# Load pieces of 256 KB and a reordered schedule in a fused attention and feed-forward kernel

## The chip, the cores and the metric

The kernel runs on one core of a Trainium2 chip. The metric is the device time of one execution in microseconds (us). A ratio between two kernels is the mean time of one kernel's fast runs over the mean time of the other's fast runs of the same rounds, so it is not quite the ratio of the medians quoted beside it. Each run is slow when it took over 1.5% more than the fastest run of the same kernel, else fast. The medians and ranges quoted are of all runs; three slow ones of the experiments are in them (a_128k 273.18, a_perm 249.43, a_tok_warm 245.64). Stretches and waits are read from one profiled execution of each kernel, which was fast except for a_128k; the span is its length.

Engines in the profile: PE is the matrix engine's matmuls, PEld its weight loads, DVE the vector engine, ACT the scalar engine, POOL the third elementwise engine, SP the engine that issues loads. A name with a q, such as ACTq, is that engine's sequencer as it issues DMAs. PEclk is the clock that the throttle granted to PE, 1.00 being full speed.

## The reference, cut to what matters

```python
# q, k, v: [4 batches, 8 heads, 768 tokens, 64], lam: [8]
for each block of 64 tokens:                       # linear attention with decay lam
    intra = (q k^T * decay mask) v
    inter = (q * lam^(pos+1)) kv_state
    out   = intra + inter
    kv_state = lam^64 * kv_state + (k * decay)^T v
x = out as [3072 tokens, 512]                      # heads side by side
h = x @ w_in                                       # [3072, 2048]   "GEMM1"
g = h + sin(alpha * h)^2 / (alpha + 1e-9)
y = g @ w_out                                      # [3072, 512]    "GEMM2"
```

## The kernel before

The kernel takes the 3072 tokens in six chunks of 512. A chunk needs four attention steps (a step is 128 tokens of two batches, four heads), 16 groups of GEMM1 and 16 groups of GEMM2. A group is four matmuls of 128x128 by 512 columns, 0.865 us at full clock. Step s reads q, k and v that SP loads as fp32; DVE and POOL scale q and k by powers of lam and round to bf16 (`prep_x`), ACT or POOL rounds v (`prep_v`); PE transposes q and k, forms the scores, and forms the output together with the running state; POOL rounds the state to bf16 (`Zs`); ACT stores the step's output as `xT`, the input of GEMM1.

The host program does not fix the order of instructions by hand. It records every operation with its reads, its writes and an assumed duration, plays them through a model of the five engines, and emits each engine's instructions in the order of the model. The program of each engine is this fixed list.

A load in the kernel before brings half of the heads of one tensor for one batch, 128 KB in packets of 512 bytes:

```python
def load(s, what="kqv", after=()):
    pair, n, hh = where(s)
    ...
    for nme in what:
        for u in range(2):                                   # two batches
            off = (((2 * pair + u) * H + HS * hh) * S + n * BL) * D
            a = bass.AP(src.tensor, off, [[2 * D, 64], [S * D, HS], [1, 2 * D]])
            op = rec_load(lambda e, ...: e.dma_start(d[half(u), :, :], a), ..., 117500, after)
```

The model of the kernel before assumes 0.25 us for an issue of SP and a rate of 270 GB/s for the loads (`issue = {"SP": 0.25, ...}`, `rate=270e3`).

The attention step works on tiles of 64 rows. The Trainium skill ("TensorEngine Tiling (Array Packing)", section "Restrictions and Gotchas", Gotcha 1) says that different row tiles cannot access the same PSUM bank at once and that software must synchronise. The kernel orders the parts of a step with fences (a fence makes a part wait until an earlier part has finished); a step has three parts in the kernel before:

```python
seqs = [block(first), block(mid), block(second)]    # cut: which matmuls go where
...
    if i == 2 and fence is not None:
        op.fence = fence                             # the third part waits for the first
```

A finished output tile of GEMM2 (128 tokens, 512 columns, 256 KB) is copied by ACT and stored with one DMA. Partition 64t+i of the tile holds token 2i+t, so the outermost dimension of the store has size 2:

```python
dst = bass.AP(out.tensor, row0 * DM, [[DM, 2], [2 * DM, 64], [1, DM]])
rec("ACT", lambda e: e.dma_start(dst, osb[o][:, :]), ...)
```

The main part, cut:

```python
for m in range(NM):
    grp_A(0, m, "ACT" if m % 5 == 4 else "POOL")              # GEMM1 of chunk 0
prep_step(4)
for i in range(16):                                           # GEMM2 of chunk 0, steps 4 to 7
    if i in B0_SEC: sec(...)
    grp_B(0, ...)
for m in range(NM):                                           # GEMM1 of chunk 1
    if m == 10: steady(6, "ACT")                              # attention inside a GEMM1 phase
    ...
for bi, (c, s4, m4) in enumerate(b_seq):                      # the rest: GEMM2, GEMM1 and attention in turns
    grp_B(c, s4, 4 * m4, 4, bank)
    for _ in range(...):
        grp_A(ca, m, ...)
        if ai % 4 == 1: steady(...)
```

Of the kernel before, what the change touches and what calls it, by code (L numbers as in the profile page):

```python
# [14 lines left out]
class Op:  # L15
    __slots__ = ("eng", "fn", "deps", "dur", "idx", "sem_after", "slot", "kslot",
                 "pos", "users", "start", "end", "nbytes", "clock", "prio", "signal", "soft", "soft_users", "fence")

    def __init__(self, eng, fn, dur, idx):
        self.eng, self.fn, self.dur, self.idx = eng, fn, dur, idx  # L20
        self.deps = set()
        self.soft = ()
        self.fence = None
        self.slot = None
        self.kslot = 0
        self.signal = False
        self.prio = idx


class Program:  # L30



    ENGINES = ("PE", "DVE", "ACT", "POOL", "SP")

    def __init__(self):
        self.ops = []
        self.writer = {}
        self.readers = {}
        self.slots = {}  # L40

    def add(self, eng, fn, dur, reads=(), writes=(), slot=None, nbytes=0, after=(), prio=None, soft=()):
        op = Op(eng, fn, dur, len(self.ops))
        if prio is not None:
            op.prio = prio
        self.ops.append(op)
        op.nbytes = nbytes
        for b in reads:
            w = self.writer.get(b)
            if w is not None:  # L50
                op.deps.add(w)
            self.readers.setdefault(b, []).append(op)
        for b in writes:
            w = self.writer.get(b)
            if w is not None and w is not op:
                op.deps.add(w)
            for r in self.readers.get(b, ()):
                if r is not op:
                    op.deps.add(r)
            self.writer[b] = op  # L60
            self.readers[b] = []
        for a in after:
            op.deps.add(a)
        op.deps.discard(op)
        op.soft = tuple(soft)
        if slot is not None:
            op.slot = slot
            self.slots[slot] = self.slots.get(slot, 0) + 1
            op.kslot = self.slots[slot]
        return op  # L70

    def schedule(self, hop=0.1, rate=270e3, begin=1.2, done=1.2):
        issue = {"SP": 0.25, "POOL": 0.8, "ACT": 0.5}
        for op in self.ops:
            op.users = []
            op.soft_users = []
        for op in self.ops:
            for d in op.deps:
                d.users.append(op)
            for d in op.soft:  # L80
                d.soft_users.append(op)
        left = {op: len(op.deps) + len(op.soft) for op in self.ops}
        ready_at = {op: 0.0 for op in self.ops}
        free = {e: 0.7 for e in self.ENGINES}
        pend = {e: [] for e in self.ENGINES}
        dma_free = 0.0
        pe_seq = [op for op in self.ops if op.eng == "PE"]
        pe_at = 0
        for op in self.ops:
            if not left[op]:  # L90
                pend[op.eng].append(op)
        order = []
        n = len(self.ops)
        while len(order) < n:
            best = None
            for e in self.ENGINES:
                if e == "PE":
                    if pe_at >= len(pe_seq):
                        continue
                    op = pe_seq[pe_at]  # L100
                    if left[op]:
                        continue
                    cand = (max(free[e], ready_at[op]), op)
                else:
                    if not pend[e]:
                        continue
                    t0 = min(max(free[e], ready_at[o]) for o in pend[e])
                    op = min((o for o in pend[e] if max(free[e], ready_at[o]) <= t0 + 1e-9),
                             key=lambda o: (o.prio, o.idx))
                    cand = (t0, op)  # L110
                if best is None or (cand[0], cand[1].idx) < (best[0], best[1].idx):
                    best = cand
            assert best is not None, "order and dependencies disagree"
            t, op = best
            e = op.eng
            if e == "PE":
                pe_at += 1
            else:
                pend[e].remove(op)
            op.start = t  # L120
            if op.slot is not None:
                free[e] = t + issue[e]
                if op.nbytes < 10000:
                    op.end = t + 2.9
                else:
                    dma_free = max(dma_free, t + begin) + op.nbytes / rate
                    op.end = dma_free + done
            else:
                op.end = t + op.dur
                free[e] = op.end  # L130
            order.append(op)
            for u in op.soft_users:
                left[u] -= 1
                ready_at[u] = max(ready_at[u], op.start)
                if not left[u] and u.eng != "PE":
                    pend[u.eng].append(u)
            for u in op.users:
                left[u] -= 1
# [74 lines left out]
def bass_lightning_attn__then__act_snake_kernel(  # L213
# [14 lines left out]
    BL = 128  # L228
# [16 lines left out]
    with es:  # L245
# [66 lines left out]
        def hold_bank():  # L312
            return idle.pop(0)
# [508 lines left out]
```

## Time and profile before

The kernel before took 280.06 us (median of three runs, 279.18 to 281.51). The span of its profiled execution is 277.9 us.

The table splits the span by what PE works on. All starts and ends are those of weight loads on PE in the trace. "Middle" is everything between GEMM1 of chunk 0 and GEMM1 of chunk 1: GEMM2 of chunk 0 and attention steps 4 to 7. "Steady" goes from the end of GEMM1 of chunk 1 to the last matmul, "tail" from there to the end of the span.

| stretch, us | before |
|---|---|
| until GEMM1 of chunk 0 | 25.6 |
| GEMM1 of chunk 0 | 16.2 |
| middle | 36.2 |
| GEMM1 of chunk 1 | 26.4 |
| steady | 156.8 |
| tail | 16.6 |

The page of the kernel before, the part with the span in 40 equal slices (one slice is 6.9 us, counted from 0 here); digits are tenths:

```profile
PE   0446999494592686978979999999999999999600
PEclk9999999959589599899999999999999999999975
GB/s 134 190 166 167 206 196 188 182 186 193 178 172 147 168 199 200 172 192 163 181 43 5 35 21 30 32 39 32 27 31 33 35 38 40 38 38 44 51 51 45
```

PE is full from slice 21 on. Before that it has holes, and in three slices its clock is at half speed. All DMA together moves 147 to 206 GB/s in slices 1 to 19; at the end the output runs at 51 GB/s with PE idle.

The view by windows of the kernel before: window, length, busy time (count) of PE, PEld, DVE, ACT and POOL, granted clock, share of the DMA engines' time, GB/s.

```profile
5.00:26.00 21.00, 8.96 (x336) 7.29 (x338) 9.52 (x14) 8.21 (x15) 13.23 (x17) 1.00 0.83 174
78.00:105.00 27.00, 18.61 (x144) 8.15 (x146) 11.22 (x17) 13.68 (x22) 14.05 (x14) 0.85 0.60 176
158.00:167.00 9.00, 8.56 (x122) 4.21 (x122) 6.95 (x10) 5.07 (x9) 5.97 (x6) 1.00 0.07 20
262.00:277.00 15.00, 0.00 (x0) 0.00 (x0) 0.00 (x0) 0.50 (x1) 0.00 (x0) 0.66 0.13 51
```

In the second line PE works 18.6 of 27 us. In the last line the DMA share of 0.13 is about two engines of sixteen.

The view of waits of the kernel before: who waits for whom, total us, times, longest us.

```profile
DVE q L409 <- DMA q<-in_q_dram: 30.7, 9, 6.3
ACT v L418 <- DMA v<-in_v_dram: 26.5, 12, 6.7
PEld PS L629 <- DVE gT L642: 15.7, 11, 7.1
```

DVE and ACT wait for loads, and PE then waits for DVE's GEMM1 results (gT) that stand behind those waits. The source line of the loads, first 24 us of the kernel before (duration of an issue in ns: least, median, most):

```profile
L333 SPq DMA_DIRECT2D k<-in_k_dram x8: 601/617/714, 0.7 to 9.4; - x8
```

One issue of 128 KB takes 0.617 us on SP, which is 0.66 us from issue to issue, so SP can ask for no more than 199 GB/s.

### The profile page before, as it was taken

The page shows a single profiled execution, that of the slowest core. Times are in us where ns is not written, and L with a number is a line of the kernel's source. Part 1 is how long each engine was busy: PE and PEld are TensorE (multiplying, and loading weights), DVE is VectorE, ACT ScalarE, POOL GpSimd, SP SyncE. Part 2 cuts the span into 40 slices and gives each one's busy share as a digit, 9 for nine tenths or more (in the row PEclk, how much of TensorE's full clock was granted, in tenths as well). Part 3 has the DMA queues.
Part 4 walks back from the last instruction along what each step waited for, and adds up shares of the span by engine and source line. Part 5 has one row for each costly group of instructions (what it writes and reads, how often), then busy time and mean ns, then how long its engine had stood idle before and what let it go on. Part 6 is the DMA issues. An engine that isn't in the chain of part 4 may idle for free.

```text
span 277.9 us, 6346 instructions
## 1 busy us (share of the span) xinstructions
PE 215.0 (77%) x2755; PEld 107.1 (39%) x2785; DVE 131.2 (47%) x181; ACT 132.0 (48%) x212; POOL 121.8 (44%) x137
## 2 busy tenths in 40 slices
PE   0446999494592686978979999999999999999600
PEld 0334444252340243543535445444444444444200
DVE  3552385332301578756778775466653444440000
ACT  5224684322433564576656566544556555541100
POOL 4656595212644463524665664344434344430000
PEclk9999999959589599899999999999999999999975
DMA  4679996666654667665610100011000111111111
GB/s 134 190 166 167 206 196 188 182 186 193 178 172 147 168 199 200 172 192 163 181 43 5 35 21 30 32 39 32 27 31 33 35 38 40 38 38 44 51 51 45
DMA packets 47243, 29.78 MB, mean 107 GB/s; under 512 B 2656, under 2 KB 44144, under 8 KB 47216
## 3 DMA queue, kind: packets, MB, share of 16 engines
q1 hardware_dynamic: 39168, 18.88, 24.1%
q0 software_dynamic: 4752, 4.19, 9.7%
q10 hardware_dynamic: 3296, 6.30, 6.7%
q8 instruction: 22, 0.36, 0.5%
q14 instruction: 5, 0.04, 0.0%
HBM read 27.28 MB, written 6.29 MB: 121 GB/s over the span
## 4 chain that ended last, share of the span: by engine, by line
PE 48%; DMA 14%; SPq 14%; DVE 11%; POOL 3%; issue 2%; ACT 2%; ACTq 0%; DVEq 0%
PE PS L652 20%; PE PS L629 19%; SPq L333 14%; DMA w<-in_moe_w_out_dram 7%; DMA q<-in_q_dram 5%; DVE gT L642 4%; PE PS L437 3%; DVE S_m L614 3%; PE PS L459 2%; DMA v<-in_v_dram 2%; DVE qkT L609 2%; PE PS L446 2%; POOL w L395 1%; POOL u L640 1%; DVE Zacc L587 1%
## 5 line engine op out<-in xcount | busy, mean ns | idle before, releaser
L640 POOL TENSOR_TENSOR u<-t 128x512 bf16<-128x512 bf16 x74 | 78.1, 1063 | 87.7 <-ACT t L633 87.5
L629 PE MATMUL PS<-xT,w 128*128 128x512 bf16 x375 | 97.0, 394 | 13.7 <-DVE gT L642 10.5
L652 PE MATMUL PS<-w,gT 128*128 128x512 bf16 x363 | 94.7, 395 | 4.3 <-issue 3.4
L642 DVE SCALAR_TENSOR_TENSOR gT<-u,r_sb,PS 128x512 bf16<-128x512 bf16 x96 | 69.9, 745 | 52.5 <-POOL u L640 45.9
L633 ACT ACTIVATE t<-PS,alpha_sb 128x512 bf16<-128x512 f32 x96 | 65.1, 686 | 55.0 <-PE PS L629 54.1
L629 PEld LDWEIGHTS PS<-xT,w 128*128 128x128 bf16 x384 | 37.7, 101 | 63.4 <-DVE gT L642 15.7
L652 PEld LDWEIGHTS PS<-w,gT 128*128 128x128 bf16 x384 | 37.0, 101 | 45.8 <-issue 5.7
L409 POOL TENSOR_TENSOR k<-k,Lk 128x512 bf16<-128x512 f32 x23 | 24.0, 1043 | 24.0 <-DMA k<-in_k_dram 18.6
L409 DVE TENSOR_TENSOR q<-q,Lq 128x512 bf16<-128x512 f32 x20 | 17.0, 850 | 33.1 <-DMA q<-in_q_dram 30.7
L614 DVE TENSOR_TENSOR S_m<-PS,mask 128x1024 bf16<-128x1024 f32 x24 | 29.1, 1218 | 4.8 <-PE PS L446 1.8
L418 ACT CAST v<-v 128x512 bf16<-128x512 f32 x24 | 14.9, 620 | 29.8 <-DMA v<-in_v_dram 26.5
L459 PE MATMUL PS<-S_m,v 64*64 64x128 bf16 x384 | 18.6, 248 | 10.0 <-ACT xT L596 5.9
L437 PE MATMUL PS<-ident,q 64*64 64x64 bf16 x384 | 14.3, 205 | 13.6 <-DVE q L409 6.8
L659 ACT COPY osb<-PS 128x512 f32<-128x512 f32 x24 | 13.9, 578 | 15.4 <-PE PS L652 15.3
L596 ACT CAST xT<-PS 128x512 bf16<-128x512 f32 x24 | 14.1, 587 | 11.4 <-DVE Zacc L587 9.5
L437 PEld LDWEIGHTS PS<-ident,q 64*64 64x64 bf16 x384 | 10.3, 116 | 23.7 <-issue 8.1
L446 PE MATMUL PS<-qkT 64*64 64x128 bf16 x384 | 18.0, 241 | 0.5 <-ACT qkT L611 0.4
L611 ACT COPY qkT<-PS 128x1024 bf16<-128x1024 bf16 x11 | 11.1, 1013 | 14.2 <-PE PS L437 13.4
L459 PEld LDWEIGHTS PS<-S_m,v 64*64 64x64 bf16 x384 | 11.5, 120 | 14.5 <-ACT xT L596 7.2
L587 DVE TENSOR_TENSOR Zacc<-PS,Zacc 128x256 f32<-128x256 f32 x16 | 6.8, 424 | 16.6 <-PE PS L437 12.3
L639 ACT ACTIVATE u<-t 128x512 bf16<-128x512 bf16 x22 | 13.8, 629 | 0.6
L437 PE MATMUL PS<-ident,k 64*64 64x64 bf16 x384 | 14.0, 203 | 0.0
(38 smaller groups left out, 103.6 us busy)
## 6 DMA issues: line engine op xcount, KB each, us to landing
k<-in_k_dram SPq DMA_DIRECT2D x48, 128.0 KB, 3.1
q<-in_q_dram SPq DMA_DIRECT2D x48, 128.0 KB, 3.4
v<-in_v_dram SPq DMA_DIRECT2D x48, 128.0 KB, 3.4
out_dram<-osb ACTq DMA_DIRECT2D x24, 256.0 KB
w<-in_moe_w_out_dram POOLq DMA_DIRECT2D x4, 512.0 KB, 17.2
w<-in_moe_w_in_dram POOLq DMA_DIRECT2D x3, 512.0 KB, 10.3
w<-in_moe_w_in_dram POOLq DMA_DIRECT2D x2, 256.0 KB, 6.4
lam_bc<-in_lam_dram ACTq DMA_DIRECT2D x1, 4.0 KB, 2.6
```

The source lines that it names most:

```text
L333: op = rec_load(lambda e, a=a, d=dst[r], u=u: e.dma_start(d[half(u), :, :], a), [f"{nme}32.{r}.{u}"], f"{nme}{r}", 117500, after)
L409: rec(eng, lambda e: e.tensor_tensor(dst[c][:, :, :], s_in, L_b, ALU.mult), 0.63 if eng == "DVE" else 1.05, reads=[f"{x}32.{r}.0", f"{x}32 ...
L418: rec("ACT", lambda e: e.copy(v2[c][:, :, :], v32[r][:, :, :].rearrange("p h (t d) -> p (h t) d", t=2)), 0.62, reads=[f"v32.{r}.0", f"v32. ...
L437: last = e.transpose(dst, src[half(u), hid(h, tt), :], ident[half(u), half(u)])
L446: return e.matmul(PS[half(u), sb_ + r, (h // 2 * 2 + tj) * 128:(h // 2 * 2 + tj + 1) * 128], qt[half(r), u, 1, h // 2, half(tj)], qt[half( ...
L459: return e.matmul(dst, v2[o % RC][half(u), hid(h, tj), :], S_m[o % RS][half(u), h % 2 ^ u, h // 2, tj, :], start=start, stop=True, skip_gr ...
L614: rec("DVE", lambda e: e.tensor_tensor(S_m[s % RS][:, :, :, :, :].rearrange("p r a t i -> p (r a) (t i)"), PS[:, sb_:sb_ + 2, :].rearrange ...
L629: last = e.matmul(PS[:, i, :], w1[:, kc, 128 * m:128 * (m + 1)], xT[x][:, kc, :], start=(kc == 0), stop=(kc == NKC - 1))
L633: rec("ACT", lambda e: e.activation(t16[tt][:, :], PS[:, i, :], ACTF.Sin, scale=alpha_sb[:, m:m + 1]), 0.7, reads=bk(i) + ["alpha"], write ...
L640: return e.tensor_tensor(u16[tt][:, :], t16[tt][:, :], t16[tt][:, :], ALU.mult)
L642: rec("DVE", lambda e: e.scalar_tensor_tensor(out=gT[g][:, m, :], in0=u16[tt][:, :], scalar=r_sb[:, m:m + 1], in1=PS[:, i, :], op0=ALU.mul ...
L652: last = e.matmul(PS[:, bank, :], gT[g][:, m, 128 * s4:128 * (s4 + 1)], w2[:, m, :], start=(m == 0), stop=(m == NM - 1))
```

## The change

Its intent is to feed PE better in the first 100 us and to waste less of the steady part.

1. A load brings all eight heads: 256 KB per DMA, half as many DMAs; SP's issue is assumed to take 0.66 us.
2. The attention step is cut into five parts around its fences instead of three.
3. Each chunk's GEMM1 is one phase on up to eight PSUM banks (PSUM is the memory that matmuls write); attention stands only in GEMM2 phases. Three of the 16 GEMM2 groups of a chunk move into the next chunk's GEMM1 phase.
4. The model that orders the instructions may now place an operation in an earlier gap of DVE, ACT or POOL (`probe`), and picks the engine that would finish first (`fastest`).

The output is left as it is. No arithmetic is taken out. The core of the diff, with cuts:

```diff
-    RL = 8
+    RL = 4
-        q32 = ring("q32", RL, [128, HS, 2 * D], F32)
+        q32 = ring("q32", RL, [128, H, 2 * D], F32)          # the same for k32, v32
 ...
-                a = bass.AP(src.tensor, off, [[2 * D, 64], [S * D, HS], [1, 2 * D]])
+                a = bass.AP(src.tensor, off, [[2 * D, 64], [S * D, nh], [1, 2 * D]])   # nh = 8
 ...
-            seqs = [block(first), block(mid), block(second)]
+                blocks = [(Ts[0] + Is[1], keys_t + keys_o, None), (Is[0] + Zz[1] + Es[1], keys_o, None),
+                          (Ts[1] + Zz[0] + Es[0] + Ss[0], keys_t + keys_o + keys_s, 0), (Ss[1], keys_s, None),
+                          (Ds[0] + Ds[1], keys_o, 2)]
 ...
+    ISSUE = {"SP": 0.66, "POOL": 0.8, "ACT": 0.66}
+    HOP, RATE, BEGIN, DONE = 0.1, 270e3, 1.2, 1.2
+    def place(self, eng, t, dur):
+        ...
+        t = self.probe(eng, t, dur)                          # first gap that is long enough
 ...
-        for bi, (c, s4, m4) in enumerate(b_seq):
-            grp_B(c, s4, 4 * m4, 4, bank)
-            for _ in range(0 if bi < START else 2 if bi in EXTRA else 1):
-                    grp_A(ca, m, "ACT" if m % 4 == 3 else "POOL")
+        for c in range(NCH):
+            for m in range(NM):
+                grp_A(c, m, every if m < 12 else ..., (SQ.get(m, "POOL"),))
+                if c > 0 and m in (3, 7, 11):
+                    grp_B(c - 1, 3, m // 4 + 1, low)
+            for i, (s4, m4) in enumerate(b_seq):
+                grp_B(c, s4, m4, ...)
+                if c > 1 and i in SEC: steady(4 * (c + 1) + SEC[i])
```

## The prediction

> **What bounds it now.** The measured 280.06 us splits, by the timeline of PE, into five stretches: 26.0 us to the first GEMM1 matmul; 78.8 us for GEMM1 of chunk 0, GEMM2 of chunk 0 with attention steps 4 to 7, and GEMM1 of chunk 1 (until 104.8); 157 us of interleaved GEMM1, GEMM2 and attention until the last matmul at 261.9; 16 us of output transfer after it; 2 us outside the span.
>
> - Stretch 2 holds 48 groups of four matmuls (0.865 us each, 41.5 us) and about 7 us of attention; about 26 us is waiting. Waits of DVE on q, ACT on v and POOL on k are 31, 27 and 19 us, longest 6 to 8 us, and the in-order engines hold up GEMM1 work queued behind them. The cause is the load queue: the SP timeline shows 0.66 us per 128 KB issue (199 GB/s) until 137 us, while a 512-byte packet takes 27 ns on one of 16 engines (303 GB/s). Loads are issue-bound.
> - Stretch 3 is PE-bound from 140 us (table by windows: PE 90 to 99% busy, clock 1.00). One period (4 GEMM1 and 4 GEMM2 groups, one attention step) is 8.76 us: 6.92 of groups, 1.64 of attention, 0.26 waiting for DVE.
> - The tail is output: 51 GB/s, DMA share 0.12, that is 2 of 16 engines; 5.1 us per 256 KB. The Trainium skill ("DMA: Bandwidth & Descriptors", section on why a DMA increments its semaphore by 16) says that the slowest dimension sets how many engines share a DMA; here it is 2. The change leaves this alone.
>
> **What changes.** No arithmetic is removed.
>
> 1. 256 KB loads: I expect the issue to stay near 0.66 us, so loads become transfer-bound at 0.87 us per piece, 303 GB/s. Weights start when v of the first block lands, about 12.5 us instead of 17.3. First GEMM1 matmul about 19.5 (saves 6.5).
> 2. Weights still need about 23.5 us, so the loads gated on them restart near 37; q for steps 4 and 5 lands about 7.5 us later. GEMM2 of chunk 0 waits some 4 us there, but the loads then stay ahead. GEMM1 of chunk 1 starts about 58.5 (78.5 before), GEMM2 of chunk 1 about 75 (104.8 before).
> 3. From there: 80 GEMM2 and 64 GEMM1 groups, 124.5 us; 18 attention steps, some partial, at 1.45 us (the five parts hide about 0.2 us of drain per step), 24 us; about 4.5 us of waits, where a phase begins or an ACT qkT copy (1.01 us after a 0.59 us xT copy) meets the next step 1.7 us later. GEMM1 phases take about 16.4 us; ACT is near 14 of it, so it should keep up. Last matmul about 228.
> 4. Tail unchanged, 16 us: four tiles of 5.1 us, the first finished 7.8 us before the end. Plus 2.
>
> Sum: 75 + 153 + 16 + 2 = **246 us**, range 236 to 257. Chances: faster by over 2% 0.97, within 2% 0.02, slower 0.01.
>
> **What would show it.** SP issue below 0.87 us, load bandwidth near 300 GB/s before 60 us; DVE waits on q below 10 us; first GEMM1 matmul near 19.5; GEMM1 of chunk 1 in about 16.5 us at clock 1.00; attention step 1.4 to 1.5 us; last matmul about 16 us before the end.
>
> **What would make it wrong.** If issue time grows with the piece (1.24 us for 256 KB), loads gain nothing: about 255. If waits of several us in GEMM2 of chunk 0 leave the clock low (matmuls at 0.43 instead of 0.216 us, as at 26 to 31 us before), add 3. If the fixed engine orders, set by assumed durations, meet late data, GEMM1 phases stretch and add 1 to 2 us per chunk. If the waits vanish, 238.

## The result and the profile after

The changed kernel took **261.02 us** (median of four runs, 260.82 to 261.4) against 279.62 of the kernel before; the ratio of the fast runs is 0.9325, 95% interval 0.9278 to 0.9372. That is faster, by 18.6 us, but 15 us slower than predicted and outside the range of 236 to 257. The result is correct; the span is 259.0 us.

| stretch, us | before | predicted | after | after less predicted |
|---|---|---|---|---|
| until GEMM1 of chunk 0 | 25.6 | 19.5 | 23.8 | +4.3 |
| GEMM1 of chunk 0 and middle | 52.4 | 39.0 | 49.6 | +10.6 |
| of this: GEMM1 of chunk 0 | 16.2 | | 14.4 | |
| of this: middle | 36.2 | | 35.3 | |
| GEMM1 of chunk 1 | 26.4 | 16.5 | 18.0 | +1.5 |
| steady | 156.8 | 153 | 150.3 | -2.7 |
| tail | 16.6 | 16 | 17.2 | +1.2 |

The prediction gave the points 19.5, 58.5, 75 and 228, from which the column follows. It named no length for the middle alone. With GEMM1 of chunk 0 as long as in the kernel before, 16.2, it leaves 39.0 - 16.2 = 22.8 us for the middle; the expectations below use that number. So the middle missed by 12.5 us. It is nearly as long as before although it holds less: 13 groups of GEMM2 instead of 16 (2.6 us). The other three stand in GEMM1 of chunk 1, where parts of two attention steps stood before.

The page after, the same three lines (one slice is 6.5 us):

```profile
PE   0448897299589999999999999999999999999400
PEclk9999999658959999999999999999999999999955
GB/s 138 226 166 172 206 206 188 227 228 220 99 154 194 224 193 186 229 134 143 97 157 150 53 51 21 34 12 49 51 17 42 3 43 51 31 40 18 51 51 44
```

PE is full from slice 12 on instead of 21. Slices 7 to 11 (45 to 78 us) hold a nearly empty one and a half-empty one, and the clock falls to half in two of them. Where loads run alone they reach 220 to 228 GB/s, not the predicted 303. The same windows after, moved with the stretches:

```profile
5.00:24.00 19.00, 9.41 (x338) 7.77 (x339) 10.84 (x16) 7.36 (x14) 11.72 (x15) 1.00 1.14 189
73.00:92.00 19.00, 18.56 (x77) 7.97 (x78) 12.14 (x19) 13.47 (x22) 11.41 (x12) 0.88 0.92 194
158.00:167.00 9.00, 9.00 (x124) 4.50 (x123) 6.80 (x10) 4.93 (x9) 5.15 (x6) 1.00 0.10 32
242.00:258.00 16.00, 0.32 (x2) 0.00 (x0) 0.00 (x0) 0.59 (x1) 0.00 (x0) 0.59 0.13 51
```

GEMM1 of chunk 1 is now PE-bound (18.56 of 19 us, with the clock at half until 77.5 us), the steady part has no waits left (9.00 of 9.00 against 8.56), and the tail is what it was. The DMA share in the first line rose from 0.83 to 1.14 while the rate rose only from 174 to 189 GB/s: more packets are under way at once, and each takes longer. From 5 to 24 us the median time of a 512-byte packet went from 27 to 42 ns in the traces.

The loads' source line after, first 24 us:

```profile
L298 SPq DMA_DIRECT2D k<-in_k_dram x4: 619/672/901, 0.7 to 4.2; - x4
L298 SPq DMA_DIRECT2D v<-in_v_dram x4: 1002/1082/1420, 7.4 to 11.0; - x4
```

The first issues of 256 KB take about as long as those of 128 KB did. The later ones take 1.08 us, which reads as the queue holding SP back: from 46 us on an issue comes every 1.12 us, and 256 KB in that time is 234 GB/s, close to the 228 that the window from 44 to 50 us shows below.

The waits after:

```profile
DVE q L381 <- DMA q<-in_q_dram: 10.0, 5, 4.8
PE PS L406 <- DVE q L381: 17.2, 3, 9.6
PE PS L428 <- POOL Zs L549: 3.2, 1, 3.2
PEld PS L577 <- DVE gT L591: 2.0, 8, 0.4
```

DVE waits 10 us for q instead of 30.7, and the weight loads of GEMM1 wait 2.0 us for gT instead of 15.7. What is left for PE is in the middle. Three views of the middle of the changed kernel follow. First the windows, then PE's two waits in the timeline (start, length, what it is, wait before it), then POOL's timeline:

```profile
38.00:44.00 6.00, 5.95 (x28) 2.51 (x26) 3.83 (x6) 1.64 (x3) 2.13 (x3) 1.00 0.90 181
44.00:50.00 6.00, 0.00 (x0) 0.00 (x0) 1.91 (x3) 0.00 (x0) 3.57 (x3) 0.73 1.22 228
50.00:56.00 6.00, 5.64 (x72) 2.90 (x72) 1.56 (x3) 2.22 (x3) 3.23 (x3) 0.50 1.23 229
```

```profile
50.23 0.43 PE L406 MATMUL PS<-ident,q 64*64 64x64 bf16 x8 [6.28 <-DVE q L381]
71.20 0.64 PE L428 MATMUL PS<-S_m,v 64*64 64x128 bf16 x16 [3.17 <-POOL Zs L549]
```

```profile
70.18 0.62 POOL L388 CAST v<-v 128x512 bf16<-128x512 f32 x1 [5.04 <-DMA v<-in_v_dram]
70.74 0.40 POOL L549 CAST Zs<-Zacc 128x256 bf16<-128x256 f32 x1
```

PE waits 6.28 us for q of step 4, which is late. The clock is then 0.50, so PE looks busy (5.64 of 6 us) while it does half the work. At 68 us it stops again for the state `Zs` of an earlier step. The data for `Zs` was there from 66.6 us; POOL sat 5.04 us on the instruction ahead of it, the rounding of a v of a later step, whose load took 13.9 us from issue to landing (median 7.1). Two more lines show what that load met, SP's two issues of q and a window in the wait:

```profile
63.08 7.61 SPq L298 DMA_DIRECT2D q<-in_q_dram  x2
69.00:70.00 1.00, 0.00 (x0) 0.00 (x0) 0.00 (x0) 0.00 (x0) 0.00 (x0) 1.00 0.13 48
```

From 68 to 71 us the core moves 48 to 50 GB/s at a DMA share of 0.13 to 0.14, two engines of sixteen; by the packets 35 to 40 of it are output and 9 to 14 loads. What is left of the loads seems to share the output's two engines while the others are idle, and SP stands on one issue for 6.42 us. The wait for q before it has another cause: it ends at 50.2 us, and the first output is written at 57.

### The profile page after: what moved, and what is told of

Same layout as the page of the kernel before. It is cut to its first block, busy times and chain, and to the rows that moved or that the text cites. A ratio compares the mean times of both kernels' runs of the same rounds, so it can differ in the third digit from the quotient of the medians.

```text
span 259.0 us, 6365 instructions
## 1 busy us (share of the span) xinstructions
PE 216.0 (83%) x2785; PEld 108.6 (42%) x2785; DVE 136.0 (53%) x190; ACT 129.2 (50%) x203; POOL 119.2 (46%) x137
## 4 chain that ended last, share of the span: by engine, by line
PE 65%; DMA 15%; SPq 9%; POOL 2%; ACT 1%; issue 1%
PE PS L614 28%; PE PS L577 28%; SPq L298 9%; DMA v<-in_v_dram 8%; DMA w<-in_moe_w_out_dram 7%; PE PS L406 3%; PE PS L438 2%; PE PS L415 2%; POOL w L359 2%; PE PS L428 2%; PE PS L451 1%; POOL w L364 1%; ACT qkT L560 0%; POOL v L388 0%; ACT xT L540 0%
## 5 line engine op out<-in xcount | busy, mean ns | idle before, releaser
L589 POOL TENSOR_TENSOR u<-t 128x512 bf16<-128x512 bf16 x66 | 67.5, 1041 | 49.8 <-ACT t L581 48.6
L577 PE MATMUL PS<-xT,w 128*128 128x512 bf16 x384 | 88.5, 385 | 2.2 <-ACT xT L540 1.4
L591 DVE SCALAR_TENSOR_TENSOR gT<-u,r_sb,PS 128x512 bf16<-128x512 bf16 x96 | 69.1, 745 | 34.9 <-POOL u L589 34.4
L406 PE MATMUL PS<-ident,q 64*64 64x64 bf16 x384 | 15.4, 212 | 17.8 <-DVE q L381 17.2
L381 POOL TENSOR_TENSOR k<-k,Lk 128x512 bf16<-128x512 f32 x16 | 17.7, 1107 | 27.4 <-DMA k<-in_k_dram 13.0
L560 ACT COPY qkT<-PS 128x1024 bf16<-128x1024 bf16 x17 | 17.3, 1016 | 16.9 <-PE PS L406 15.8
L621 ACT COPY osb<-PS 128x512 f32<-128x512 f32 x24 | 14.2, 591 | 16.2 <-PE PS L614 13.6
L428 PE MATMUL PS<-S_m,v 64*64 64x128 bf16 x384 | 14.6, 239 | 3.2 <-POOL Zs L549 3.2
L381 DVE TENSOR_TENSOR q<-q,Lq 128x512 bf16<-128x512 f32 x16 | 11.5, 741 | 10.0 <-DMA q<-in_q_dram 10.0
L438 PE MATMUL PS<-qkT,Zs 64*64 64x128 bf16 x160 | 15.6, 234 | 0.4
L549 POOL CAST Zs<-Zacc 128x256 bf16<-128x256 f32 x16 | 8.0, 498 | 16.5 <-DVE Zacc L547 16.5
L415 PE MATMUL PS<-qkT 64*64 64x128 bf16 x384 | 13.5, 238 | 1.1 <-ACT qkT L560 0.4
L451 PE MATMUL PS<-v,k 64*64 64x64 bf16 x320 | 11.5, 207 | 1.7 <-issue 1.7
```

Of the source, the lines that this page charges most:

```text
L381: rec(eng, lambda e: e.tensor_tensor(dst[c][:, :, :], raw(src, s), L_b, ALU.mult), dur, reads=reads, writes=writes)
L406: last = e.transpose(dst, src[half(u), hid(h, tt), :], ident[half(u), half(u)])
L415: return e.matmul(PS[half(u), sb_ + r, (h // 2 * 2 + tj) * 128:(h // 2 * 2 + tj + 1) * 128], qt[half(r), u, 1, h // 2, half(tj)], qt[half( ...
L428: return e.matmul(dst, v2[o % RC][half(u), hid(h, tj), :], S_m[o % RS][half(u), h % 2 ^ u, h // 2, tj, :], start=start, stop=True, skip_gr ...
L438: return e.matmul(dst, Zs[(o - 2) % 3][half(r), u, h // 2, :], qkT[o % RQ][half(r), u, 0, h // 2, :], start=start, stop=True, skip_group_c ...
L577: last = e.matmul(PS[:, i, :], w1[:, kc, 128 * m:128 * (m + 1)], xT[x][:, kc, :], start=(kc == 0), stop=(kc == NKC - 1))
```

## The experiments

Sixteen kernels ran. The theories, as the expectations name them in words: (1) the loads land late in the middle, because their rate is lower than assumed and because the output, which uses two DMA engines, slows them; the same output makes the tail; (2) the clock that halves after PE's first wait; (3) the order of the engines, or the five-part block, itself takes the time. "After" is the changed kernel, and the table has the stretches of the table above, without GEMM1 of chunk 0. Unless an experiment says otherwise, the order of all other instructions on every engine was compared with that of the kernel that it changes and is the same; in a_3part PE's order inside a step differs, and in a_tok_best a few preparations move with the loads.

| run (us) | time, range | ratio to before | until GEMM1 | middle | GEMM1 of chunk 1 | steady | tail |
|---|---|---|---|---|---|---|---|
| after | 261.02, 260.82–261.4 | 0.9325 | 23.8 | 35.3 | 18.0 | 150.3 | 17.2 |
| a_out16 | 250.78, 249.82–252.97 | 0.9039 | 24.7 | 32.0 | 16.0 | 158.5 | 4.7 |
| b_out16 | 256.57, 256.22–257.42 | 0.9242 | 26.5 | 34.3 | 18.5 | 156.1 | 4.7 |
| a_warm | 262.2, 261.73–262.34 | 0.9436 | 23.4 | 35.5 | 18.1 | 150.9 | 17.2 |
| a_3part | 260.09, 259.68–260.54 | 0.9363 | 23.9 | 34.4 | 18.9 | 148.4 | 17.2 |
| a_128k | 266.55, 265.88–273.18 | 0.9561 | profile slow | | | | |
| a_perm (wrong) | 246.87, 244.56–249.43 | 0.8823 | 23.3 | 33.4 | 16.0 | 152.8 | 3.8 |
| b_perm (wrong) | 254.95, 253.88–256.69 | 0.9159 | 26.3 | 33.0 | 18.1 | 155.0 | 3.7 |
| a_perm_last (wrong) | 247.28, 246.32–247.7 | 0.8872 | 23.3 | 34.6 | 17.0 | 150.5 | 3.7 |
| a_rows | 337.46, 336.24–339.58 | 1.2128 | | | | | |
| a_rowsp | 319.7, 317.06–319.98 | 1.1488 | | | | | |
| a_tok | 246.38, 246.12–248.79 | 0.8875 | 23.4 | 32.7 | 16.0 | 153.0 | 3.8 |
| a_tok_warm | 245.03, 241.98–245.64 | 0.8764 | 24.9 | 29.9 | 16.0 | 152.1 | 3.8 |
| **a_tok_best** | **242.47**, 241.12–244.45 | 0.8714 | 23.5 | 31.7 | 16.1 | 151.4 | 3.8 |
| a_tiny (wrong) | 254.46, 253.99–256.05 | 0.9149 | 24.2 | 28.6 | 16.0 | 150.4 | 17.3 |
| a_tiny_warm (wrong) | 255.83, 254.46–257.09 | 0.9157 | 23.5 | 26.7 | 22.5 | 150.3 | 17.2 |
| a_all (wrong) | 240.01, 238.51–240.79 | 0.8582 | 23.5 | 27.7 | 16.0 | 150.7 | 3.8 |

The code of GEMM1 of chunk 0, which the table leaves out, is the same in all runs with the changed order but a_rows and a_rowsp, yet it takes 13.9 to 16.4 us there: in some executions PE starts it at half pace, one matmul in 0.43 us, in others not. Differences of 1 to 2 us between two profiles are therefore not read as effects.

### The output on sixteen engines: a_out16 and b_out16

The Trainium skill ("DMA: Bandwidth & Descriptors", section "Why a DMA increments its semaphore by 16 and not by 1") says that the number of engines of a DMA is the largest number up to 16 that divides the sizes of both sides' slowest dimension. Here that is 2, which agrees with the DMA share of 0.13 and the 51 GB/s of the tail. Two stores of 64 rows each have a slowest dimension of 64:

```diff
-                dst = bass.AP(out.tensor, row0 * DM, [[DM, 2], [2 * DM, 64], [1, DM]])
-                rec("ACT", lambda e: e.dma_start(dst, osb[o][:, :]), ...)
+                for t in range(2):
+                    dst = bass.AP(out.tensor, (row0 + t) * DM, [[2 * DM, 64], [1, DM]])
+                    rec("ACT", lambda e, ...: e.dma_start(dst, osb[o][half(t), :]), ...)
```

> The changed kernel with each 256 KB output split into two transfers of 64 rows, whose slowest dimension is 64 instead of 2; the order of all other instructions on every engine is the same. Theory 1 (contention): the output occupies two of the sixteen DMA engines that every load also needs, so loads fall from 228 to about 80 GB/s while output is written, and v of the fifth load block, issued at 56 and landed at 70 us, holds the Zs copy behind it on POOL and PE with it. Then v lands about 60, the 3.2 us wait of PE on Zs at 68 to 71 us goes, GEMM1 of chunk 1 starts near 69 instead of 73.4 and not cold (3.5 instead of 5.6 us for its first four groups): 5 to 6 us less in the middle. Besides, the tail falls from 16.7 to about 5 us. Total near 244. Rival (the loads are late because of their gate on the weights and of the queue order, not because of the output): only the tail falls, by about 11 us: near 250, with GEMM1 of chunk 1 still at 73.

> The kernel before with the output split in the same way. Theory 1: its tail falls from 16 to about 5 us, and its loads, which have 151 GB/s while output is written and 193 otherwise, are not slowed; stretch 2 (26 to 104.8 us) waits for loads, so it shortens by 3 to 6 us: 263 to 266. Rival: tail alone, 269.

Measured: both are correct. The tail falls from 17.2 to 4.7 us. In the changed kernel the middle falls from 35.3 to 32.0 and GEMM1 of chunk 1 from 18.0 to 16.0, but the steady part grows by 8.2 us. So the total is the 250 that the rival theory expected, while the middle moved as the first theory said. The timeline of ACT in the steady part of a_out16 shows part of what was added there:

```profile
137.91 0.61 ACT L621 COPY osb<-PS 128x512 f32<-128x512 f32 x1
138.55 1.90 ACTq L627 DMA_DIRECT2D out_dram<-osb  x2
```

ACT spends 1.90 us on issuing two stores, and the next `xT` copy starts at 142.32 us, behind them and the next pair; the attention step that needs it keeps PE waiting for 1.70 us. PE waits 6.4 us in this steady part (waits over 0.15 us) and not at all in that of the changed kernel. Of these, 3.6 us go back to late copies of ACT and 2.2 us are waits for which the profile names nothing (see a_all). Besides, the clock is at half from 100.2 to 103.6 us.

On the kernel before, the same edit alone gives 256.57 us. This is 22 us less than the 278.77 of the runs beside it, more than the whole change gained (18.6) and more than both expectations (263 to 266, or 269). Besides the tail, GEMM1 of chunk 1 falls from 26.4 to 18.5 us. The waits of that stretch, which the change removed by its new order, therefore hung on the output too. How fast q, k and v arrive, from the packets in the traces, in stretches of 1 us without weight traffic until the last load (median in GB/s, number of stretches; the output is busy where it moves over 25 GB/s):

| kernel | output idle | output busy |
|---|---|---|
| before | 191 (63) | 145 (37) |
| b_out16 | 194 (82) | 142 (16) |
| after | 226 (51) | 84 (52) |
| a_128k (slow profile) | 188 (66) | 119 (51) |
| a_tok (below) | 222 (62) | 173 (13) |

The right column depends on the count: with any output at all it is 140, 146, 104, 119 and 203. The expectations quote the earlier count (193 and 151, 83). In the changed kernel 19 of the 52 stretches are under 50 GB/s, like the one shown above, in the kernel before 1 of 37. In b_out16 the loads are no faster beside the output than before, but the output is busy in 16 stretches instead of 37.

The same skill page ("Queues, rings and completion order") says that each DMA engine takes packets from the queues in turn. That fits: a load's data is spread over all 16 engines, so it is complete only when the two that also carry the output are done, and from 68 to 71 us the trace shows just that remainder (9 to 14 GB/s). The runs show the loss and that it goes with the two-engine store. Why the changed kernel loses more (to 84) than the kernel before (to 145) no run tests; a full queue would fit, for SP stands up to 6.42 us on one issue there and at most 1.74 us before.

### The clock: a_warm

```diff
+                    if i == 5:
+                        warm(26, 4)       # 26 matmuls of zeros into bank 4, in the wait before step 4
```

> The changed kernel with 26 dummy matmuls (5.6 us) on PE in its 6.3 us wait before attention step 4, so that it stays warm; nothing else moves. Rival theory 2 (the cold clock is what costs in GEMM2 of chunk 0): the groups at 51 to 60 us take 0.86 instead of 1.8 us, and the gain of about 4 us reaches the end: 257. Theory 1 (a late v load ends the stretch): PE is faster from 50 to 60 us, reaches step 7 earlier and waits longer for the same v; GEMM1 of chunk 1 still starts near 73: 260 to 261.

Measured: 262.2 us, not faster. The fillers do keep the clock up until 64.7 us (in the changed kernel it is at half from 46.8 to 60.4), but PE waits 2.28 us at 63.3 us, with nothing named, and then 3.67 us for `Zs` at 71.9 us, and the middle is 35.5 as before. What ended the middle in the changed kernel was the late v, whatever the clock. The cold clock was therefore hidden behind the data; the runs below show what it is worth when the data is there.

### The five parts: a_3part

```diff
-                blocks = [(Ts[0] + Is[1], ...), (Is[0] + Zz[1] + Es[1], ...), ..., (Ds[0] + Ds[1], ...)]
+                blocks = [(first, both, None), (mid, keys_s, None), (second, both, 0)]   # as in the kernel before
```

> The changed kernel with the attention block of before, in three parts. My prediction gave the five parts 0.2 us per step: 18 steps, 3.6 us slower, 264.6. The traces say a step takes 1.59 us after and 1.64 before: about 1 us slower, 262.

Measured: 260.09 us, ratio 0.9363 against 0.9325 for the changed kernel in its own rounds, whose intervals overlap: the totals show no gain from the five parts. The step itself shows a loss. The 1.59 and 1.64 us of the expectation are read from matmul records, and in the profiles of a_3part and of the kernel before the first matmul after each step is missing, which makes the step look one matmul, 0.216 us, longer. No weight load is missing: from the last load of one group to the first of the group after a full step it is 1.84 us before, 1.83 in a_3part and 2.01 in the changed kernel. So the five parts take about 0.17 us more per step, and the steady part of a_3part is 1.9 us shorter (148.4 against 150.3).

### The piece size: a_128k

```diff
-            for u in range(2):
+            for u, h0 in [(u, HS * p) for u in range(2) for p in parts]:      # 128 KB pieces again
```

> The changed kernel with its loads in 128 KB pieces, as before the change; same orders on all other engines. With issues of 0.66 us loads have at most 199 GB/s instead of 228 while no output runs: first GEMM1 matmul 2 us later (25.8), loads for steps 4 to 7 another 2 us. While output runs, loads had 151 GB/s before and 83 after the change. If the piece size is the reason, it returns to about 150, v of the fifth block lands earlier and the wait for it goes: total 258 to 261, no worse than with 256 KB. If not, 264 to 266.

Measured: 266.55 us; its three other runs are 265.9 to 266.9, and the profiled run 273.2. The large pieces alone are worth 5 to 7 us of the 18.6 (5.2 by the fast runs' times, 6.6 by the ratios). The other 12 to 13 come from parts 2 to 4 of the change, of which part 2 gains nothing; the split between parts 3 and 4 was not measured. The 84 GB/s beside the output are not the reason for a loss, as the first expectation had it: with small pieces the loads reach 119 there, and the time is the one expected otherwise (264 to 266).

### One store of contiguous rows: a_perm, b_perm, a_perm_last, then a_tok

If `xT` is stored in token order, a tile's partitions are its rows in order, and one store has 128 rows as its slowest dimension:

```diff
+                    xo = xT[x][:, 2 * ho:2 * ho + 2, col:col + 256].rearrange("p a (u i t) -> p a u t i", u=2, t=2)
+                    xi = PS[:, ob:ob + 2, 0:256].rearrange("p u (a t i) -> p u a t i", a=2, t=2)
-                dst = bass.AP(out.tensor, row0 * DM, [[DM, 2], [2 * DM, 64], [1, DM]])
+                dst = bass.AP(out.tensor, row0 * DM, [[DM, 128], [1, DM]])
```

> The changed kernel with the columns of xT written in token order (same ACT copies, another access pattern), so that an output tile is 128 contiguous rows and goes out as one 256 KB transfer on sixteen engines: the cure of a_out16 without its 24 added issues on ACT. In a_out16 the stretch from GEMM2 of chunk 1 to the last matmul took 157.9 us against 150.3 in the changed kernel. If that loss was the added issues (they stood before xT copies on ACT, once for 1.9 us), it goes: GEMM2 of chunk 1 starts near 88.5, last matmul near 239, tail 4 us, total 245. If it was something else that sixteen-engine output does, the total stays at 250.

> The kernel before with the same edit. If output on two engines was what held up its loads, it repeats b_out16: 255 to 257. The difference to a_perm is what the change is worth once output is out of the way: about 10 us, if a_perm comes to 245; of the 18.6 us that it brought, the rest was then contention that it happened to escape.

> The changed kernel with the edit of a_perm for the last chunk of 512 tokens alone: the outputs written beside loads stay on two engines. Contention theory: the middle stays as it was (GEMM1 of chunk 1 at 73.4, last matmul near 242), only the tail falls, from 16.7 to about 4: 248 to 249. If a_perm is not faster than this, output beside loads cost nothing.

Measured: all three gave wrong results (relative error 1.0037 for the first, 0.417 for the one that does it in the last chunk only). The fault is in the edit shown: the destination walks its dimensions as a, u and the source as u, a. Their times are still those of the intended traffic. a_perm takes 246.87 us and a_perm_last 247.28, so nearly all of the gain on the changed kernel is the tail; having the earlier output on 16 engines as well takes 2.2 us off the middle and GEMM1 of chunk 1 (33.4 for 34.6, 16.0 for 17.0) and gives 2.3 back in the steady part, 1.7 of it in PE waits for which the profile names nothing. b_perm takes 254.95 us: with the output on 16 engines in both kernels, the rest of the change is worth 8.1 us instead of 18.6, less than the 10 that was expected.

With the dimensions in the same order (`"p a (u i t) -> p u a t i"`):

> The changed kernel with the attention output stored in token order by the ACT copy (both access patterns now walk their dimensions in the same order) and one output DMA of 128 contiguous rows. Theory (the earlier wrong result was the mismatch of the two patterns, and the output on two engines costs the tail and some of the middle): correct, 245 to 248 us, tail about 4, middle about 33.5, second GEMM1 stretch 16. Rival (the ACT copy cannot walk four free dimensions): wrong result again.

Measured: correct, 246.38 us, as expected within 1 us in every stretch. The ACT copy of `xT` takes 737 ns instead of 586. That the mismatch was the fault is now shown, since nothing else differs from a_perm.

### The same order taken inside the matmul: a_rows and a_rowsp

Before the fault was found, the order was moved into GEMM1's access patterns, which costs no instruction.

```diff
 # a_rows: moving operand read with a stride of 64 elements
+                    xs = xT[x][:, kc, :].rearrange("p (s t i) -> p s i t", s=4, t=2)
 # a_rowsp: result written to PSUM with a stride of 2 elements
+                    ys = PS[:, i, :].rearrange("p (s i t) -> p s t i", s=4, t=2)
```

> The changed kernel with one output DMA per tile whose 128 rows are contiguous, so that it can use 16 engines; the token order is restored by reading the columns of xT in another order as GEMM1's moving operand, so the number of instructions on every engine is unchanged. Theory 1 (the output on two engines slows the loads in the middle and makes the tail): the result is correct, the tail falls from 17 us to about 4, the stretch between GEMM1 of chunk 0 and of chunk 1 from 35.3 to about 33.5, GEMM1 of chunk 1 from 18.0 to 16; 245 to 247 us, as the wrong-result run of the same DMA took. Rival 1 (the wrong result of the earlier permuted runs comes from the output DMA's row order and not from the four-dimensional copy): wrong result again. Rival 2 (a strided moving operand streams slower): a GEMM1 matmul takes clearly more than 0.216 us and the steady part grows by more than 5 us.

> The same output DMA, but the column order is changed where GEMM1 writes PSUM and the moving operand is read in blocks of 64 columns. Theory 1: correct, 245 to 247 us, within 1 us of the run that permutes the moving operand. Rival 2 (strided access in the matmul costs time): whichever of the two strides costs shows a GEMM1 matmul of clearly more than 0.216 us in one run and not in the other.

Measured: both correct, both far slower, 337.46 and 319.7 us. Theory 1 was right about the result and the transfer, and the strides cost much more than that gained. Groups by line, GEMM1's matmuls in the kernel after, in a_rows and in a_rowsp (total busy us, then mean ns of one with its pipeline; the busy total over the 384 matmuls is the time that each adds):

```profile
L577 PE MATMUL PS<-xT,w 128*128 128x512 bf16 x384 | 88.5, 385 | 2.2 <-ACT xT L540 1.4 <-issue 0.8
```

```profile
L578 PE MATMUL PS<-xT,w 128*128 128x512 bf16 x384 | 189.0, 645 | 1.4 <-ACT xT L540 1.4
```

```profile
L579 PE MATMUL PS<-xT,w 128*128 128x512 bf16 x375 | 167.7, 638 | 4.1 <-ACT xT L540 2.5 <-issue 1.3 <-DVE gT L593 0.2
```

A matmul adds 88.5/384 = 0.230 us in the changed kernel, 0.492 with the strided moving operand, 0.437 with the strided result (167.7/384; nine of the 384 records are missing). The Trainium skill ("SBUF — State Buffer", section "Door 1: The DMA port swizzle (why `[64,N]` ≈ `[32,N]`)") says that accesses within one 16-byte line of SBUF run at full bandwidth, eight bf16 elements, and that any non-contiguous access to PSUM slows matmuls because its lines are 8 bytes. Both runs agree.

### What the clock and the order of loads are worth once the output is out of the way: a_tok_warm, a_tok_best

```diff
 # a_tok_warm: a_tok and 26 fillers before step 4
 # a_tok_best: a_tok, 18 fillers, and
-        for x in "kqv":
-            for d in (2, 3):
-                load(d, x, after=[gate])
+        for d, x in ((2, "k"), (2, "q"), (3, "k"), (3, "q"), (2, "v"), (3, "v")):
+            load(d, x, after=[gate])
```

> The same with 26 filler matmuls in the wait before attention step 4. Theory 2 (once the data is no longer late, the halved clock is what is left in the middle): the middle falls by 4 to 6 us against the run without fillers, 240 to 243 us. Theory 1 or 3 alone (data or order still ends the middle): within 1.5 us of it, as the fillers did on the changed kernel as it is.

> The same with 18 fillers and the loads of the third and fourth block ordered k, q of one, k, q of the other, then v: q of step 4 comes one 512 KB pair earlier. Theory 1: the wait before attention step 4 falls from 6.3 us to about 4, and the middle by another 2; 238 to 241 us. Theory 3: no change.

Measured: the fillers shorten the middle from 32.7 to 29.9 us, half of what was expected. The total moves by 1.4 us, which the spread of the runs (242.0 to 245.6 here, 246.1 to 248.8 for a_tok) hardly resolves. a_tok_best takes 242.47 us, a little above the expected 238 to 241. PE's waits for q fall to 0.84 and 0.89 us, but the time comes back as other waits: from 44 to 68 us the DMA share stays at 1.14 to 1.23 and the rate at 218 to 285 GB/s, which points to the load queue; and at 62.6 us PE waits 1.90 us with nothing named. This is the fastest correct version: 36 us under the kernel before (ratio 0.8714, 0.8641 to 0.8787) and 18.5 under the changed one.

### Taking the late data away: a_tiny, a_tiny_warm, a_all

To separate late data from the clock and from the order, the loads of the third and fourth block (a block is q, k and v of two steps) were shrunk to 64 packets each. The preparations of steps 4 to 7 read a tile of constants instead, so the result is wrong. No wait was removed; its cause was.

```diff
+                n1 = 1 if d in (2, 3) else nh
-                a = bass.AP(src.tensor, off, [[2 * D, 64], [S * D, nh], [1, 2 * D]])
+                a = bass.AP(src.tensor, off, [[2 * D, 64], [S * D, n1], [1, 2 * D]])
+            if s // 2 in (2, 3):
+                t = {s // 2 % RL: fake}          # a tile that holds 0.01
```

> The changed kernel with the loads of the third and fourth block shrunk to 64 packets each, and the preparation of steps 4 to 7 reading a constant tile in their place: a wrong result on purpose, the order of instructions on every engine unchanged. Theory 1 (late data makes the middle long): the wait of 6.3 us before attention step 4 and the wait for the state copy of 3.2 us go, the clock stays up, and the middle falls from 35.3 to 23 to 26 us, close to the 22.8 of the prediction; total about 249 to 252. Theory 3 (the order itself): the middle stays over 32 us and the total within 3 us of 261.

Measured: the middle falls from 35.3 to 28.6 us, between the two expectations. So 6.7 us of the 12.5 go with the loads of these two blocks: with their lateness, and with the room that they take from the loads behind them, which the run does not separate. The clock did not stay up. The view by windows of a_tiny:

```profile
44.00:47.00 3.00, 1.73 (x8) 0.59 (x6) 3.00 (x3) 0.00 (x0) 3.00 (x3) 1.00 0.18 49
47.00:50.00 3.00, 2.23 (x51) 1.49 (x52) 1.86 (x2) 1.46 (x3) 2.89 (x3) 0.91 0.49 133
50.00:53.00 3.00, 2.94 (x38) 1.45 (x36) 0.69 (x1) 1.65 (x4) 1.03 (x1) 0.50 1.10 220
59.00:62.00 3.00, 2.67 (x60) 1.66 (x60) 1.57 (x3) 0.59 (x1) 0.00 (x0) 0.50 0.47 140
```

In the first line there is no late data any more, and DVE and POOL are busy for all of 3.00 us: the preparations of steps 4 and 5 themselves make PE wait, 1.83 us. After that the clock is at half speed for 13.7 us (49.4 to 63.1) with PE almost always busy. So a_tiny_warm adds 12 fillers in that wait:

> The run with the two shrunk load blocks, with 12 filler matmuls in its wait of 1.8 us before attention step 4; a wrong result on purpose again. If the halved clock is what is left of the middle: the granted clock stays at 1.00 from 44 to 68 us, and the middle falls from 28.6 to 23 to 25 us, near the prediction's 22.8; total about 249 to 251. If the order of the engines is what is left: the middle stays over 27 us although the clock is full, with waits in its place. If the clock halves in spite of the fillers, the run says nothing.

Measured: the clock stays at 1.00 through the middle, which falls to 26.7 us, under the "over 27" of one theory and above the "23 to 25" of the other. But GEMM1 of chunk 1 grows from 16.0 to 22.5 us, and the total is no better. The timeline of DVE there:

```profile
74.01 0.69 DVE L386 TENSOR_TENSOR q<-q,Lq 128x512 bf16<-128x512 f32 x1 [3.31 <-DMA q<-in_q_dram]
75.22 4.16 DVE L596 SCALAR_TENSOR_TENSOR gT<-u,r_sb,PS 128x512 bf16<-128x512 bf16 x6
```

PE came earlier to GEMM1, and six `gT` operations of GEMM1, ready long before, stand in DVE's queue behind a preparation whose q landed late, beside the output on two engines. PE waits 3.66 us for the first of them, and the clock is then at half until 81.4 us. The last of the series takes all three away at once: shrunk loads, 12 fillers, and the one store of a_tok.

> Two shrunk load blocks, 12 filler matmuls and the one-DMA output in token order, all at once; a wrong result on purpose. If the three causes are the whole: full clock, middle 23 to 25 us, second GEMM1 stretch 16, its end at about 79 us, total 234 to 238. If the order of the engines holds a part: the middle stays over 26 us with waits of the engines for each other and not for loads.

Measured: 240.01 us, over the expected 234 to 238. GEMM1 of chunk 1 is 16.0, the tail 3.8, and the middle 27.7, over the expected 23 to 25. So 4.9 us over the 22.8 are left without late loads of those two blocks, and with a full clock but for 60.9 to 64.3 us. Most of it can be named in PE's timeline of a_all. Each of the first five lines is one group of GEMM2, with one attention call between two groups; then come a wait whose releaser the profile does not name (it says "issue") and, from the page, the queue that brings instructions:

```profile
47.72 1.04 PE L622 MATMUL PS<-w,gT 128*128 128x512 bf16 x4
49.57 1.04 PE L622 MATMUL PS<-w,gT 128*128 128x512 bf16 x4
51.65 1.04 PE L622 MATMUL PS<-w,gT 128*128 128x512 bf16 x4
53.72 1.04 PE L622 MATMUL PS<-w,gT 128*128 128x512 bf16 x4
55.66 1.04 PE L622 MATMUL PS<-w,gT 128*128 128x512 bf16 x4
59.88 0.27 PE L443 MATMUL PS<-qkT,Zs 64*64 64x128 bf16 x3 [2.30 <-issue]
q8 instruction: 22, 0.36, 0.7%
```

From group to group it is (55.66 - 47.72)/4 = 1.99 us; less the group's own 0.865, an attention call takes 1.12 us at full clock, although each does only some of a step's three jobs (transposes, scores, output). Eight calls are 9.0 us. The prediction's 22.8 us, less its 4 us of waiting and 13 groups (11.2 us), left 7.6 for them. The rest of the 27.7 us, as an estimate from the same timeline: 2.7 before step 4, where the fillers stand and DVE and POOL prepare steps 4 and 5, the 2.30 of the wait, 1.3 lost to the clock and 0.8 for `xT` at the end.

The author left the wait of 2.30 us open. The kept traces narrow it. Queue q8 brings 22 packets of 16 KB in every run. The 18 profiles hold 29 matmul waits of PE over 0.6 us for which nothing is named, and 28 of them end 1.2 to 1.6 us after such a packet has landed; here it landed at 58.4 us, and PE went on at 59.9. That PE waits for its next instructions is the likely reading; no run tests it. The changed kernel has two such waits, 1.70 us before GEMM1 of chunk 0 and 0.81 us in it.

## Why the prediction was wrong, point by point

The direction was right (0.97 on faster), and these steps held. The issue of a large piece does not take longer while the queue has room (0.62 to 0.67 us). The steady part is PE-bound and lost its waits (150.3 against 153 predicted). That the two are so close is partly luck: the 4.5 us of waits in the forecast did not come, and what is left beside the 124.5 us of groups, attention, took 25.8 us instead of 24. The tail stayed (17.2 of span against 16). PE's waits for `gT` in GEMM1 of chunk 1 all but vanished. A cold clock in the middle was named as a risk, with 3 us.

These steps failed:

1. *"loads become transfer-bound at 0.87 us per piece, 303 GB/s"*. They run at 226 GB/s alone. The 303 was worked out from a packet time (27 ns) that was read while SP held the engines back; with full queues the median is 42 ns. GEMM1 starts at 23.8 instead of 19.5 us (+4.3): v of the first block lands at 15.7 instead of 12.5, which is 3.2 of it, and one of the waits with nothing named, 1.70 us, lies there too.
2. *"GEMM2 of chunk 0 waits some 4 us there, but the loads then stay ahead"*. This is the main term: 35.3 instead of 22.8 us for the middle. PE waits 6.28 us for q and 3.17 for the state behind a late v. The first wait goes with the rate (step 1): the loads restart at 39.4 us instead of 37, q of step 4 lands 10.0 us later instead of 7.5, and no output is written yet. After that the loads do not stay ahead, because GEMM2 of chunk 0 starts to produce output beside which the loads fall to 84 GB/s at the median. That output costs the middle 1.2 us by a_perm against a_perm_last and 3.3 by a_out16. By the runs: shrinking two load blocks gives 6.7 us back, holding the clock up another 1.9, and 3.9 remain over 22.8 in a_tiny_warm and 4.9 in a_all, where attention calls at 1.12 us, the preparation of steps 4 and 5 and a wait with nothing named stand. These parts are read one after the other from single profiles; taken in another order they would come out differently, because one wait hides the next, as the fillers that gained nothing on the changed kernel show.
3. *"the five parts hide about 0.2 us of drain per step"*. They hide none: by the weight loads a step is about 0.17 us longer with them (2.01 against 1.83 in a_3part), and undoing them does not change the total beyond the noise. The 1.64 us of attention that the prediction saw before hold a matmul whose record is missing.
4. *"Tail unchanged"* was right, yet the prediction treated the two-engine output as a matter of the tail alone. It did not ask what those two engines do to the loads, which spread over them.

The terms add up: +4.3 at the start, +10.6 in GEMM1 of chunk 0 and the middle (+12.5 in the middle, the rest being the assumed 16.2 against 14.4), +1.5 in GEMM1 of chunk 1 (its first 4.1 us are at half clock, a loss of about 2 us), -2.7 in the steady part and +1.2 in the tail make 14.9 of the 15.0 us.

Where the expected gain went: of some 34 us, 15 are missing, and nearly all of that is lost before GEMM1 of chunk 1 starts, to loads that are slower than assumed and to what waits behind them. What the new order saved in waits for `gT` was in part a cost of the output's two engines: with the old order, the store alone takes 7.9 us off GEMM1 of chunk 1. One edit to the output store, on the kernel before, takes 22 us, more than the whole change.

What stays open: why the loads lose more beside the output in 256 KB pieces (to 84 GB/s) than in 128 KB pieces (to 119, in a slow profile, and 145); whether PE waits for instructions where the profile names nothing, as the packets suggest; what the room freed by the shrunk loads is worth apart from their lateness; and how the 12 to 13 us of the order split between longer GEMM1 phases and filled gaps.

## What to carry to other kernels

A packet time read while the queue is not full is no bandwidth: before the rate of a saturated queue is predicted, find a window in the trace where the DMA share is over 1, and read the rate there. The kernel before had one, with weights under way: 26 to 42 us, share 1.20, 199 GB/s. When a store uses few DMA engines, count its cost also in the loads that spread over the same engines, and when engines run in a fixed order, look for the ready work that stands behind a late load. A wait that hides another gives nothing when it alone is removed, so take the causes away together before one of them is called worthless.

## What the Trainium skill lacked or had wrong

- "DMA: Bandwidth & Descriptors" lists bandwidth by transfer size for a single stream (section "Bandwidth") but not what many queued 256 KB loads with 512-byte packets reach: 226 GB/s here at a DMA share of 1.22, with a median of 42 ns per packet, against 27 ns when the issuing engine is the limit.
- The same page tells how few engines a store gets from a slowest dimension of 2 and that engines take packets from the queues in turn, but gives no size for what such a store costs other DMAs: loads fell from 226 to 84 GB/s at the median while it ran, and with it on 16 engines they had 173.
- The same page says that splitting a transfer into two half-partition DMAs is not worth the trouble (section "Rules for kernel authors"), because both halves use all 16 engines anyway. It does not name the exception: a store whose slowest dimension is 2 does not, and splitting it is worth 22 us on the kernel before. It costs ACT up to 1.90 us for the two issues, and one store of 128 contiguous rows avoids that.
- "TensorE: Matmul & The Clock Gate" (Part 1) gives an idle window of about 3.4 us for the clock to halve; a later section says that frequent short idles make it oscillate, without a size. In a_tiny the clock was at 0.50 from 49.4 us on although PE's longest wait before it was 1.83 us; in a_tok_best it was at 0.51 from 53 to 56 us after two waits of under 0.9 us each, among small 64x64 matmuls. In a_tok_warm a wait of 2.82 us at 66.1 us did not halve it.
- "SBUF — State Buffer" names the slowdown of strided access without a size for a matmul: a 128x512 matmul adds 0.492 us with a moving operand at a stride of 64 bf16 elements and 0.437 us with a PSUM result at a stride of two fp32 elements, against 0.230.
